# Score and expert products issued as 64-row halves of two tiles, with the dots' small operations on GpSimd

## The chip, the core and the metric

The kernel runs on one core of one Trainium2 chip. The metric is the time of one execution on the device, in microseconds (us). A core has five engines with instruction queues of their own: TensorE (PE in the profile, its weight loads PEld), VectorE (DVE), ScalarE (ACT), GpSimd (POOL) and SyncE (SP, which issues most DMAs here).

## The reference

The input x (2048 rows of 512) is normalised by row, and two branches are added to it. Branch A is attention with 32 heads of 16 columns that share one key and one value head. Branch B sends each row through 4096 experts: per head the two best of 64 keys on each of two sides are found, their four sums ranked, and the two best sums choose two experts.

```python
xn = _layernorm(x, axis=-1)
return x + _A_ref(xn, A_wq, A_wk, A_wv, A_wo) + _B_ref(xn, B_w_q, B_k1, B_k2, B_u, B_v)

# A: scores = einsum("bhqd,bkd->bhqk", q, k) * Dh**-0.5; softmax; times v; times wo
# B, per row n and head h (32 heads, dk = 128, E = 64, K = 2):
s1 = jnp.einsum("nhd,ed->nhe", q1, k1); s2 = jnp.einsum("nhd,ed->nhe", q2, k2)
i1 = jnp.argsort(-s1, axis=-1)[..., :K]; i2 = jnp.argsort(-s2, axis=-1)[..., :K]
cand = t1[..., :, None] + t2[..., None, :]         # 4 sums, of which the best 2 are kept
g = _softmax(top_s, axis=-1)
act = _gelu(jnp.einsum("nd,nhkd->nhk", xf, u[top_e]))
out = jnp.einsum("nhk,nhk,nhkd->nd", g, act, v[top_e])
```

## The kernel before

**Tiles and precision.** Rows are worked on in 16 tiles of 128. Products that must be exact are made of a high and a low part: an operand is split into two fp32r halves, and three of the four cross products are summed (`TERMS`), so a product over 512 columns takes 4 x 3 = 12 matmuls into one PSUM tile.

**Start.** Rows are normalised, transposed (`XT`), and projected to q, k and v.

**The attention loop.** Everything after that stands in one loop of 256 turns plus a tail (`att_steps`, one turn for each d). A turn issues, in this order on PE: two score products of two key blocks (`scores`, L326, 64 rows each, two side by side), the sixteen small products of the turn before with v (`pv`, L340, 32 columns each, four side by side), the second two score products, and then the fill. ScalarE takes the exponential of each score tile (L329, four per turn).

**The fill.** PE's other work is a generator (`score_thread`), which `run_scores` advances in each turn until the units it has paid for reach `done0 + (FILL - done0) * (d + 1) / half`, or 4 units in one turn (`MOST`). A matmul of the fill costs 0.235 units (`UNIT`), a full-precision block of the output projection (`block_out`) 3.6. The generator gives up control after every three matmuls. In order it contains:

- Expert scores (`item`, psc, L531): 32 items of four row tiles, 12 matmuls each. `wp_make` prepares the weights for the first eight; later items read them back (`wp_read`). DVE scans each tile with max and max_index (L544, L546); after four tiles `batch` turns the result into expert numbers and gates, partly on GpSimd (L590 to L638).
- Rows 0 to 1023 (phases 0 and 1) use their experts by gathering: `gather` (GpSimd, L976) fetches a row of u and v for each of 128 rows, `dot` (DVE, L988) makes the activation, `add` (DVE, L1023) accumulates. Between these stand three small operations on DVE per four dots (L997 to L999, queued in `CHAIN`), a tanh on ScalarE (L1004, issued in the middle of the next turn) and one more DVE operation (`weigh`, L1011).
- Rows 1024 to 2047 (phases 2 and 3) are worked through dense (`dense`): one-hot products make a gate matrix (pg, L815), and then for each of 32 blocks of 128 experts there is an activation product (pact, L733, 12 matmuls) and, after each second block, four output products (pout, L861, 6 matmuls each). The expert weights are read as fp32 and split into two halves on ScalarE and DVE (L697, L698).

**Order.** The lists `ON_ACT`, `LAST`, `LATER`, `BEHIND`, `STORES` hold functions that issue work at a set place in a later turn: `mid` runs them between the products with v and the second scores. PSUM gives three buffers to all fill tiles (`xtile`), two to attention scores. The scheduler keeps each engine's instructions in the order in which the program issues them.

Of the kernel before, what the change touches and what calls it, by code (L numbers as in the profile page):

```python
# [23 lines left out]
P = 128  # L24
# [31 lines left out]
def tile_kernel(ctx, tc, x, wq, wkv, wo, wqT, kT, uv, ub, vb, out):  # L56
# [70 lines left out]
    XT, XN, ACC, XP = {}, {}, {}, [None]  # L127
# [43 lines left out]
    def transpose_group(g):  # L171
        first = g < 1
        XT[g] = []
        for k in range(KC):
            if first:
                xt = big.tile([P, 2, 512], F32R, name="xt", tag="xt", bufs=4)
# [7 lines left out]
            XT[g].append(xt)  # L184
            if not first:
                nc.sync.dma_start(d_xt[g - 1][k], raw(xt[:]))
# [6 lines left out]
    def project_kv(g):  # L193
        p = stile("pkv")[:, 0, :]
        n = 0
        for k in range(KC):
            for a, b in TERMS:
                w = (wkv_h, wkv_l)[a]
                nc.tensor.matmul(p[:32, :], w[:, k, :], XT[g][k][:, b, :], start=n == 0, stop=n == 11)
# [21 lines left out]
    def project_q(g, wqs):  # L221
        pq = xtile("pqs")
        for r in range(KC):
            p = stile("pq")[:, 0, :]
            n = 0
            for k in range(KC):
                for a, b in TERMS:
                    nc.tensor.matmul(p, wqs[k][:, a, r * P:(r + 1) * P], XT[g][k][:, b, :],
# [282 lines left out]

    def item(n_, ti, make=()):
# [5 lines left out]
        if jb == 0:  # L518
            m8 = small.tile([P, BT, 8, 8], F32, name="m8", bufs=1)
            i8 = small.tile([P, BT, 8, 8], U32, name="i8", bufs=1)  # L520
            M8[ph, c, b], I8[ph, c, b] = m8, i8
        m8, i8 = M8[ph, c, b], I8[ph, c, b]
        p = xtile("psc")

        last = ti == TPH - 1
        more = nc_ is not None and not (ph >= NSP and c == NC - 1)
        read = more and n_ + 1 >= NC
        n = 0
        for k in range(KC):
            for a, bb in TERMS:  # L530
                nc.tensor.matmul(p, XT[g][k][:, a, j * P:(j + 1) * P], WC[n_][k][:, bb, :],  # L531
                                 start=n == 0, stop=n == 11)
                n += 1
            if read and ti == 0 and k < 2:
                wp_read(n_ + 1, range(2 * k, 2 * k + 2))
            if last and more and nph != ph:
                load_phase2_xt(nph, k)
# [5 lines left out]
        for s in range(8):  # L543
            nc.vector.max(m8[:, jb, s, :], p[:, s * E:(s + 1) * E])  # L544
        for s in range(8):
            nc.vector.max_index(i8[:, jb, s, :], m8[:, jb, s, :], p[:, s * E:(s + 1) * E])  # L546
        if jb == BT - 1:
            batch(ph, c, b)
# [14 lines left out]
    def batch(ph, c, b):  # L563
# [25 lines left out]
        G_ = nc.gpsimd  # L589
# [66 lines left out]
    def dense(DG, after):  # L656
# [4 lines left out]
        def fetch(b):  # L661
            if b < NB and b not in raws:
                rw = big.tile([P, 2, 512], F32, name="rw", tag="wqt", bufs=2)
                nc.sync.dma_start(rw[:, 0, :], ub[b])
                nc.sync.dma_start(rw[:, 1, :], vb[b])
# [27 lines left out]
        splits, halved, multiplied, halves = {}, set(), [0], {}  # L693
# [7 lines left out]
        def split(b):  # L701
            if b < NB:
                if b not in raws:
                    run(STORES)
                us = None if b < 2 else halves.pop(b) if b in halves else half_split(b, 0)
                splits[b] = us, half_split(b, 1)
                behind(lambda: halved.add(b))
                raws.pop(b)

        def later_split(b):  # L710
            def go():
                split(b)
                store(lambda: fetch(b + 2))
            on_act(go)
# [6 lines left out]
        fetch(0)  # L721
        fetch(1)
        yield 0.0
        early = []
        on_act(lambda: early.extend(half_split(b, 0) for b in range(2)))
# [3 lines left out]
        def activations(b, us, p):  # L729
            n = 0  # L730
            for k in range(KC):
                for a, c in TERMS:
                    nc.tensor.matmul(p, us[:, a, k * P:(k + 1) * P], XT[DG][k][:, c, :],  # L733
                                     start=n == 0, stop=n == 11)
                    n += 1
                yield k

        def first(b):
            p = xtile("pact")
            for k in activations(b, early[b], p):  # L740
                if k < KC - 1:
                    yield 3 * UNIT
            g, y = gate_rows(b), hh[:, b, :]
            nc.scalar.activation(y, p, AF.Square, scale=C_CUB ** 0.5)
            nc.scalar.copy(g, p)
            nc.vector.scalar_tensor_tensor(y, y, C_IN, p, op0=OP.add, op1=OP.mult)

            def go():
                nc.scalar.activation(y, y, AF.Tanh)
                behind(lambda: nc.vector.scalar_tensor_tensor(y, y, 1.0, g, op0=OP.add, op1=OP.mult))  # L750

            LATER.append(go)
            yield 3 * UNIT
# [11 lines left out]
        yield from first(0)  # L765
        rest_of_first = first(1)
        yield from islice(rest_of_first, 2)
# [37 lines left out]
        yield from rest_of_first  # L805
        onehot(1)
        for q in range(NQ):
# [28 lines left out]
            if q in (NQ - 16, NQ - 12):  # L836
                later_split((NQ - 16, NQ - 12).index(q))
            if q == NQ - 3:
                on_act(lambda: halves.__setitem__(2, half_split(2, 0)))
            if q == NQ - 3:  # L840
                quiet[0] = 3
            if q == NQ - 2:
                dense_on[0] = 3
                on_act(lambda: halves.__setitem__(3, half_split(3, 0)))
                later_split(2)
            if q == NQ - 1:
                later_split(3)
            yield 2.0
        held, ready, used = [], [], [0]

        def sums():

            used[0] += 2
            if formed[0] < used[0]:
                flush()
            for j in range(GT):
                p = xtile("pout")
                n = 0
                for wd, vs in ready:
                    for a, c in TERMS:  # L860
                        nc.tensor.matmul(p, wd[0][:, a, j * P:(j + 1) * P], vs[:, c, :], start=n == 0, stop=n == 5)  # L861
                        n += 1
                acc = ACC[GT * DG + j]
                nc.vector.tensor_add(acc, acc, p)  # L864
                yield 6 * UNIT

        stt = nc.vector.scalar_tensor_tensor
        for b in range(NB):
            wd = []
            if b > 1:  # L870
                if b not in halved:

                    yield None
                if b not in halved:
                    flush()
                p = xtile("pact")
                for k in activations(b, splits[b][0], p):
                    if k == 0:
                        store(lambda b=b: fetch_gates(b + 1))
                        if b % 2 == 0 and b > 2:  # L880
                            later_split(b + 2)
                        if b == 2:

                            store(load_totals)
                    if k == KC - 1 and b == NB - 1 and after is not None:
                        wp_read(after, range(2))
                    if b == NB - 1 and after is not None:
                        load_phase2_xt(SEQ[after][0], k)
                    if k < KC - 1:
                        yield 3 * UNIT  # L890

                if b not in fetched:
                    if b > 3 and formed[0] < b - 2:
                        flush()
                    run(STORES)
# [476 lines left out]
```

## Time and profile before

| what | value |
|---|---|
| median of 3 runs | 1929.25 us (1923.3 to 1929.8) |
| the profiled execution | 1925.78 us |
| its span | 1924.1 us |
| mean granted PE clock | 0.981 |
| busy: PE, DVE, ACT, POOL | 97%, 85%, 67%, 36% of the span |
| DMA | 491 MB, mean 255 GB/s |

The profile is of one execution; its span runs from the first to the last instruction, and the profiled time is 1.7 us longer. Groups of instructions are told by line, engine and operation, with busy time, mean duration of one and the idle time before them. Matmuls overlap each other, so the mean duration of one is longer than the distance between two.

### The profile page before, as it was taken

The page shows a single profiled execution, that of the slowest core. Times are in us where ns is not written, and L with a number is a line of the kernel's source. Part 1 is how long each engine was busy: PE and PEld are TensorE (multiplying, and loading weights), DVE is VectorE, ACT ScalarE, POOL GpSimd, SP SyncE. Part 2 cuts the span into 40 slices and gives each one's busy share as a digit, 9 for nine tenths or more (in the row PEclk, how much of TensorE's full clock was granted, in tenths as well). Part 3 has the DMA queues.
Part 4 walks back from the last instruction along what each step waited for, and adds up shares of the span by engine and source line. Part 5 has one row for each costly group of instructions (what it writes and reads, how often), then busy time and mean ns, then how long its engine had stood idle before and what let it go on. Part 6 is the DMA issues. An engine that isn't in the chain of part 4 may idle for free.

```text
span 1924.1 us, 34929 instructions
## 1 busy us (share of the span) xinstructions
PE 1863.8 (97%) x10990; PEld 991.8 (52%) x10990; DVE 1634.0 (85%) x6381; ACT 1294.2 (67%) x1803; POOL 700.8 (36%) x920
## 2 busy tenths in 40 slices
PE   6979999999999999999999999999999999999998
PEld 3634444555555554555555554555555455555553
DVE  6627787989998977999999897899988779999994
ACT  3346666655557887787877555555578777888873
POOL 1203334434452223343444444355422134344430
PEclk9989999999999899999999999999988899999999
DMA  7857789787773778888999987876736778899882
GB/s 274 315 186 278 266 272 301 279 296 251 249 246 122 233 240 249 253 288 270 287 300 309 362 287 237 280 256 220 242 105 220 249 215 292 271 284 286 282 277 84
DMA packets 234395, 491.13 MB, mean 255 GB/s; under 512 B 93396, under 2 KB 93396, under 8 KB 234204
## 3 DMA queue, kind: packets, MB, share of 16 engines
q0 software_dynamic: 73728, 268.47, 42.0%
q1 hardware_dynamic: 159240, 219.56, 34.9%
q8 instruction: 88, 1.44, 0.3%
q10 hardware_dynamic: 1236, 0.82, 0.1%
q14 instruction: 103, 0.84, 0.1%
HBM read 427.41 MB, written 56.07 MB: 251 GB/s over the span
## 4 chain that ended last, share of the span: by engine, by line
PE 85%; DMA 3%; ACT 3%; DVE 1%; issue 1%; SPq 0%; DVEq 0%; ACTq 0%
PE pv L340 24%; PE psc L531 18%; PE sc L326 17%; PE pact L733 9%; PE pout L861 9%; PE pg L815 3%; PE pwo L433 2%; ACT pt L329 2%; PE pw L486 1%; DMA wqt<-in_wqT_dram 1%; DMA dinv<-rc 1%; DMA wk<-dw 1%; PE pwt L493 0%; PE pwl L408 0%; DMA qa<-dqh 0%
## 5 line engine op out<-in xcount | busy, mean ns | idle before, releaser
L329 ACT ACTIVATE pt<-sc 128x1024 f32<-128x1024 f32 x1024 | 993.7, 1026 | 461.9 <-PE sc L326 460.5
L976 POOL DMA_INDIRECT g<-in_uv_dram,idx x512 | 556.8, 1087 | 1002.0 <-DVE xa L1023 531.0
L340 PE MATMUL pv<-pt,vaug 128*32 128x512 f32 x4096 | 516.4, 623 | 0.0
L531 PE MATMUL psc<-wk,xt 128*128 128x512 f32 x1536 | 388.7, 401 | 4.1 <-DVE wk L496 3.5
L326 PE MATMUL sc<-qa,kaug 64*128 64x512 f32 x2048 | 384.2, 451 | 8.6 <-ACT pt L329 8.4
L1023 DVE SCALAR_TENSOR_TENSOR xa<-g,w,xa 128x512 f32<-128x512 f32 x512 | 371.7, 744 | 0.1
L988 DVE CUSTOM_DVE_ANT_0 g<-g,xa 128x512 f32<-128x512 f32 x512 | 335.5, 681 | 7.4 <-DMA g<-in_uv_dram,idx 7.4
L531 PEld LDWEIGHTS psc<-wk,xt 128*128 128x128 f32 x1536 | 277.9, 188 | 107.7 <-issue 37.5
L326 PEld LDWEIGHTS sc<-qa,kaug 64*128 64x128 f32 x2048 | 155.9, 185 | 329.3 <-ACT pt L329 218.8
L340 PEld LDWEIGHTS pv<-pt,vaug 128*32 128x32 f32 x4096 | 109.6, 111 | 257.0 <-issue 255.4
L546 DVE FIND_INDEX8 i<-m,psc 128x8 uint32<-128x64 f32 x1024 | 206.3, 220 | 0.0
L733 PE MATMUL pact<-xt,wk 128*128 128x512 f32 x768 | 195.9, 400 | 0.0
L861 PE MATMUL pout<-wk,wd 128*128 128x512 f32 x768 | 194.8, 401 | 0.2 <-DVE wd L919 0.2
L544 DVE MAX8 m<-psc 128x8 f32<-128x64 f32 x1024 | 146.2, 213 | 41.1 <-PE psc L531 40.3
L861 PEld LDWEIGHTS pout<-wk,wd 128*128 128x128 f32 x768 | 140.8, 188 | 47.3 <-DVE act L988 5.5
L733 PEld LDWEIGHTS pact<-xt,wk 128*128 128x128 f32 x768 | 139.4, 188 | 48.5 <-issue 17.5
L698 DVE TENSOR_TENSOR wk<-rw,wk 128x512 fp32r<-128x512 f32 x128 | 84.8, 683 | 9.7 <-ACT wk L697 9.7
L864 DVE TENSOR_TENSOR da<-da,pout 128x512 f32<-128x512 f32 x128 | 82.8, 679 | 10.1 <-PE pout L861 10.0
L783 DVE TENSOR_TENSOR oh<-oh 128x2048 f16<-128x2048 f16 x64 | 78.0, 1219 | 0.8 <-ACT oh L759 0.6
L815 PEld LDWEIGHTS <-oh 128*128 128x128 f16 x1024 | 68.4, 162 | 13.8 <-issue 6.4
L1011 DVE SCALAR_TENSOR_TENSOR w<-gth,ga 128x4 f32<-128x4 f32 x128 | 20.4, 159 | 64.5 <-ACT gth L1004 64.0
L815 PE MATMUL pg<-oh 128*128 128x32 f16 x1024 | 73.5, 247 | 0.6 <-DVE oh L786 0.5
(159 smaller groups left out, 1411.1 us busy)
## 6 DMA issues: line engine op xcount, KB each, us to landing
wk<-dw SPq DMA_DIRECT2D x96, 512.0 KB
wqt<-in_wqT_dram SPq DMA_DIRECT2D x32, 512.0 KB
dw<-wk SPq DMA_DIRECT2D x32, 512.0 KB
rw<-in_ub_dram SPq DMA_DIRECT2D x64, 256.0 KB
rw<-in_vb_dram SPq DMA_DIRECT2D x64, 256.0 KB
gy<-dg SPq DMA_DIRECT2D x64, 256.0 KB
qa<-dqh SPq DMA_DIRECT2D x128, 64.0 KB
g<-in_uv_dram,idx POOLq DMA_INDIRECT x512, 6.0
```

The costliest lines, as they stand in the source:

```text
L326: nc.tensor.matmul(p[:, b, :], kaug[o:o + 64, kc * P:(kc + 1) * P], QA[u][o:o + 64, i, :], start=True, stop=True)
L329: nc.scalar.activation(pt, p, AF.Exp, scale=SCALE)
L340: nc.tensor.matmul(PV[u][32 * j:32 * j + 32, :], vaug[:, kc, :], pt[:, b, :], start=kc == 0, stop=kc == 15)
L531: nc.tensor.matmul(p, XT[g][k][:, a, j * P:(j + 1) * P], WC[n_][k][:, bb, :], start=n == 0, stop=n == 11)
L544: nc.vector.max(m8[:, jb, s, :], p[:, s * E:(s + 1) * E])
L546: nc.vector.max_index(i8[:, jb, s, :], m8[:, jb, s, :], p[:, s * E:(s + 1) * E])
L733: nc.tensor.matmul(p, us[:, a, k * P:(k + 1) * P], XT[DG][k][:, c, :], start=n == 0, stop=n == 11)
L815: nc.tensor.matmul(p[:, i * NB:(i + 1) * NB], oa[:, :, i], ob[:, :, i], start=True, stop=True)
L861: nc.tensor.matmul(p, wd[0][:, a, j * P:(j + 1) * P], vs[:, c, :], start=n == 0, stop=n == 5)
L976: nc.gpsimd.indirect_dma_start(out=gt, out_offset=None, in_=uv, in_offset=bass.IndirectOffsetOnAxis(ap=IDX[ph, c, ti][:, s:s + 1], axis=0))
L988: nc.vector.tensor_tensor_reduce(u, u, XN[TPH * ph + ti], scale=1.0, scalar=0.0, op0=OP.mult, op1=OP.add, accum_out=a[:, i:i + 1])
L1023: nc.vector.scalar_tensor_tensor(acc, v, w[:, i:i + 1], acc, op0=OP.mult, op1=OP.add)
```

## The change

**Half products.** Fill tiles are no longer issued as the generator goes. `item`, `first`, `sums` and the dense loop now yield a `Tile`: its list of matmuls and a function for afterwards (`done`). `run_scores` collects the tiles of a turn and hands them to `products`. That takes the last tiles of the turn, up to 12 matmuls, and issues for each matmul only the product over rows 0 to 63; beside these, one for one, it issues the products over rows 64 to 127 of the tiles that were left half done by the turn before. Tiles that do not fit, or are marked `alone`, follow as whole products. A tile of halves is therefore complete, and its `done` issued, one fill later. Score items 0 to 6 keep the old form. A turn's fill now ends at a tile's end, no longer after three matmuls.

**Dense weights.** The u half of a block is split two blocks ahead of its use, in one buffer with the v half of the block two before. The output products of a pair of blocks come as two for each of the two following blocks, no longer four in a row.

**Loads.** `XT` is one set of four tiles for all phases; a phase's last item reloads each tile's 128 columns (`load_xt`) when that tile is done. `wp_read` moves into the first tile's `done`.

**Chain.** The three DVE operations per four dots become four on GpSimd, `weigh` becomes two on GpSimd, and the tanh is issued at the end of the turn that made the dots. `CHAIN` is gone. In the last item of a dense phase, the part of `batch` that was on GpSimd runs on DVE.

```diff
+        def mm(self, i, half=None):
+            if self.p is None:
+                self.p = xtile(self.name)
+            w, v = self.steps[i]
+            n = len(self.steps)
+            if half is None:
+                nc.tensor.matmul(self.p, w, v, start=i == 0, stop=i == n - 1)
+            else:
+                o = slice(64 * half, 64 * half + 64)
+                nc.tensor.matmul(self.p, w[o], v[o], start=i == 0 and half == 0, stop=i == n - 1 and half == 1)
...
+    def products(tiles):
+
+        n, first = 0, []
+        while tiles and not tiles[-1].alone and n + len(tiles[-1].steps) <= 12:
+            n += len(tiles[-1].steps)
+            first.insert(0, tiles.pop())
+        a = [(t, i, 0) for t in first for i in range(len(t.steps))]
+        b = [(t, i, 1) for t in HALF for i in range(len(t.steps))]
+        if first or any(t.alone and t.steps for t in tiles):
+            for i in range(max(len(a), len(b))):
+                for run_ in (a, b):
+                    if i < len(run_):
+                        t, k, half = run_[i]
+                        t.mm(k, half)
+            for t in HALF:
+                t.done(t.p)
+            HALF[:] = first
+        for t in tiles:
+            t.whole()
...
+            if read and ti == 0:
+                wp_read(n_ + 1)
+            if more and nph != ph:
+                load_xt(nph, j)
...
+        tile_ = Tile("psc", steps, done)
+        if n_ >= NC - 1:
+            yield tile_
+            return
...
-        G_ = nc.gpsimd
+        G_ = V if ph >= NSP and c == NC - 1 else nc.gpsimd
...
+            return Tile("pact", activations(us_of.pop(b)), done, b == 1)
...
+            if b % 2 == 0 and b > 3:
+                yield from ready(b - 4)
+                yield from sums(b - 4, (2, 3))
+            if b % 2 and b > 1:
+                yield from ready(b - 3)
+                yield from sums(b - 3, (0, 1))
...
-            CHAIN.append(lambda: stt(q, a, C_CUB, a, op0=OP.mult, op1=OP.mult))
-            CHAIN.append(lambda: stt(y, q, C_IN, a, op0=OP.add, op1=OP.mult))
-            CHAIN.append(lambda: nc.vector.tensor_tensor(out=pairs(ga), in0=pairs(a), in1=gg, op=OP.mult))
+            V = nc.gpsimd
+            V.tensor_mul(q, a, a)
+            V.tensor_scalar(q, q, C_CUB, C_IN, op0=OP.mult, op1=OP.add)
+            V.tensor_mul(y, q, a)
+            V.tensor_tensor(out=pairs(ga), in0=pairs(a), in1=gg, op=OP.mult)
...
-            nc.vector.scalar_tensor_tensor(w, th, 1.0, ga, op0=OP.add, op1=OP.mult)
-            WT[n] = w
+        nc.gpsimd.tensor_mul(w, th, ga)
+        nc.gpsimd.tensor_add(w, w, ga)
+        WT[n] = w
...
-            if n + 1 < len(SEQ) and SEQ[n + 1][0] != ph and not (ph >= NSP and c == NC - 1):
-                yield None
...
+            if not isinstance(cost, float):
+                assert key is None
+                tiles.append(cost)
+                cost = len(cost.steps) * UNIT
             spent[0] += cost
+        products(tiles)
...
-                tanhs(d_next[0])
                 run(ON_ACT)
...
             att_steps(d, mid, fill)
+            tanhs(d_next[0])
```

More of the change, by code (lines that the diff above doesn't have):

```diff
@@ L542, in item @@
                 yield from islice(make, 1)
[L543 to L548, printed above, removed]
+        done(tile_.p)
         yield 3 * UNIT
@@ L804, in dense @@
         onehot(0)
-        yield from rest_of_first
         onehot(1)
```

330 lines of the change are left out of this document (148 added, 182 removed).

## The prediction

> **What bounds the kernel.** I read the page's busy shares and its chain first, then a table by stage, then the timeline of TensorE (PE) over single turns of the attention loop.
>
> ```profile
> span 1924.1 us, 34929 instructions
> PE 1863.8 (97%) x10990; PEld 991.8 (52%) x10990; DVE 1634.0 (85%) x6381; ACT 1294.2 (67%) x1803; POOL 700.8 (36%) x920
> PE 85%; DMA 3%; ACT 3%; DVE 1%; issue 1%; SPq 0%; DVEq 0%; ACTq 0%
> ```
>
> PE is busy 97% of the span and carries 85% of the chain that ended last. The table (columns: PE, PEld, DVE, ACT, POOL, clock, DMA share, GB/s) covers score fill, dense fill, score fill, dense fill:
>
> ```profile
> 353.00:590.00 237.00, 235.39 (x1345) 130.49 (x1341) 220.48 (x1415) 137.26 (x168) 112.54 (x201) 1.00 0.76 265
> 744.00:1066.00 322.00, 321.39 (x1818) 177.09 (x1818) 297.58 (x695) 252.19 (x356) 132.45 (x118) 1.00 0.89 285
> 1066.00:1400.00 334.00, 333.14 (x1873) 179.18 (x1877) 301.06 (x1845) 193.90 (x237) 153.86 (x251) 1.00 0.78 266
> 1560.00:1890.00 330.00, 329.70 (x1863) 180.42 (x1855) 305.45 (x716) 257.09 (x365) 130.60 (x115) 1.00 0.86 271
> ```
>
> PE is full in all four; VectorE (DVE) follows at 90 to 93%. So a turn lasts as long as PE's work in it. One turn with 15 fill products, the next with 18; then a turn without fill:
>
> ```profile
> 513.38 0.73 PE L326 MATMUL sc<-qa,kaug 64*128 64x512 f32 x4
> 514.04 1.92 PE L340 MATMUL pv<-pt,vaug 128*32 128x512 f32 x16
> 515.89 0.73 PE L326 MATMUL sc<-qa,kaug 64*128 64x512 f32 x4
> 516.56 3.70 PE L531 MATMUL psc<-wk,xt 128*128 128x512 f32 x15
> 520.18 0.73 PE L326 MATMUL sc<-qa,kaug 64*128 64x512 f32 x4
> ...
> 523.36 4.38 PE L531 MATMUL psc<-wk,xt 128*128 128x512 f32 x18
> 527.67 0.73 PE L326 MATMUL sc<-qa,kaug 64*128 64x512 f32 x4
> 528.33 1.06 PE L340 MATMUL pv<-pt,vaug 128*32 128x512 f32 x8
> ```
>
> ```profile
> 373.67 1.92 PE L340 MATMUL pv<-pt,vaug 128*32 128x512 f32 x16
> ...
> 377.22 0.51 PE L326 MATMUL sc<-qa,kaug 64*128 64x512 f32 x2 [0.97 <-ACT pt L329]
> 378.14 0.50 PE L326 MATMUL sc<-qa,kaug 64*128 64x512 f32 x2 [0.41 <-ACT pt L329]
> 378.57 0.64 PE L340 MATMUL pv<-pt,vaug 128*32 128x512 f32 x4
> ```
>
> The first turn is 520.18 - 513.38 = 6.80 us, the second 527.67 - 520.18 = 7.49: three products more cost 0.69, so a full 128-row fill product is 0.228. Without its 15 products a turn is 6.80 - 3.42 = 3.38. Of that, sixteen pv are four groups of (1.92 - 1.06)/2 = 0.43, together 1.72; eight sc are four pairs, and a second pair adds 0.73 - 0.50 = 0.23, together 0.92. What is left, 0.74, belongs to the four places where the row or column form of the products changes (sc to pv, pv to sc, sc to fill, fill to sc): 0.185 each. The turn without fill lasts 378.57 - 373.67 = 4.90, not 3.38: there PE waits for ScalarE's exponentials (ACT pt). 4.90 is a floor under every turn.
>
> **The change, part by part.**
>
> *Mode changes removed.* A fill that holds only half products keeps the 64-row form of sc on both sides: two of the four changes go, 2 x 0.185 = 0.37. A fill that also runs a whole tile keeps both. How often? A turn's budget is (948 - 17)/256 = 3.64 units at 0.235 per product, 15.5 products, and a tile is now taken whole. Score tiles have 12 products (2.82 units), so a fill takes one or two, 1.29 on average. The 25 items in the new form have 100 tiles: 78 fills, 55 with a single tile, which then runs as halves only. In the dense stage a block is one pact (12) and two pout (6 each); by the budget the fills go round through [pout, pout], [pact, pout], [pout, pact]. Only the first has no whole tile. Worked through turn by turn this gives 20 and 21 such fills. Sum: 96 x 0.37 = -36 us. Items 0 to 6 stay as they are.
>
> *Halves without a partner.* `products` takes the last tiles up to 12 products as first halves and runs them beside the second halves left from the fill before; the shorter list leaves slots with one half. In the round above the lists are 12 and 12, 6 and 12, 12 and 6: 36 slots, and 18 whole products beside them, for what was 48 products. Six slots are lost per three fills: 168 in the two dense stages, 6 more where `first(1)` is alone. A lone half is not in the trace.
>
> ```profile
> L531 PE MATMUL psc<-wk,xt 128*128 128x512 f32 x1536 | 388.7, 401 | 4.1 <-DVE wk L496 3.5
> L326 PE MATMUL sc<-qa,kaug 64*128 64x512 f32 x2048 | 384.2, 451 | 8.6 <-ACT pt L329 8.4
> L531 PEld LDWEIGHTS psc<-wk,xt 128*128 128x128 f32 x1536 | 277.9, 188 | 107.7 <-issue 37.5
> L326 PEld LDWEIGHTS sc<-qa,kaug 64*128 64x128 f32 x2048 | 155.9, 185 | 329.3 <-ACT pt L329 218.8
> ```
>
> From below it is 0.114, half a product; from above 0.228. A 64-row product is not shorter than a 128-row one (451 ns against 401) and its weight load is as long (185 against 188), so I take 0.228: 174 x 0.228 = +40 us; with the low end +20.
>
> *Pairs.* 2,112 slots hold halves. The sc pair at 0.23 says that a slot with two halves costs what a whole product costs: 0. The low end is the load alone, 0.185: -91. The high end, 0.24, is +25.
>
> *ScalarE's floor.* In the dense stages ACT is busy 252.2/322 = 78% of turns of about 6.9 us, 5.4 us; four exponentials are 4.1, so 1.3 of other work stands on top of what the 4.90 floor holds. A turn of twelve slots would need 3.38 + 12 x 0.228 - 0.37 = 5.75 on PE, less than 4.90 + 1.3. Of the 0.37 saved there between none and all is lost; I take 0.15 in 41 turns, +6 (0 to +15).
>
> *Chain on GpSimd (POOL).* Three small DVE operations and `weigh` become six POOL ones, per four slots, 128 times.
>
> ```profile
> L1011 DVE SCALAR_TENSOR_TENSOR w<-gth,ga 128x4 f32<-128x4 f32 x128 | 20.4, 159 | 64.5 <-ACT gth L1004 64.0
> L999 DVE TENSOR_TENSOR ga<-act,gg 128x4 f32<-128x4 f32 x128 | 20.2, 158 | 0.0
> L998 DVE SCALAR_TENSOR_TENSOR gy<-gq,act 128x4 f32<-128x4 f32 x128 | 20.2, 158 | 1.6
> L997 DVE SCALAR_TENSOR_TENSOR gq<-act 128x4 f32<-128x4 f32 x128 | 20.1, 157 | 0.4
> L630 POOL TENSOR_TENSOR e<-e,cond 128x16 f32<-128x16 f32 x32 | 13.5, 421 | 2.5
> L976 POOL DMA_INDIRECT g<-in_uv_dram,idx x512 | 556.8, 1087 | 1002.0 <-DVE xa L1023 531.0
> ```
>
> DVE loses 81 us of work and 64 of waiting for the tanh; PE sets the turn, so this is worth 0. POOL gains 768 x 0.42 = 323 us beside 701, which fits its idle time, but two orders change. (The last item's list of 13 operations goes the other way, twice, to DVE: 26 x 0.16 = 4 us, beside PE, 0.) First, ScalarE's tanh now stands before the next turn's exponentials and waits for four POOL operations. Second, the two POOL operations that form w stand behind the fill's `batch` on POOL.
>
> ```profile
> 503.97 0.08 DVE L988 DVE_READ_ACCUMULATOR2_ANT act<- 128x1 f32 x1
> ...
> 510.19 1.40 DVE L1023 SCALAR_TENSOR_TENSOR xa<-g,w,xa 128x512 f32<-128x512 f32 x2
> ```
>
> ```profile
> 507.18 1.94 ACT L329 ACTIVATE pt<-sc 128x1024 f32<-128x1024 f32 x2 [2.35 <-PE sc L326]
> ```
>
> ```profile
> 508.13 0.31 POOL L590 CAST fi<-i 128x64 f32<-128x64 uint32 x1 [2.20 <-DVE i L546]
> ...
> 514.09 0.46 POOL L638 TENSOR_TENSOR da<-hi,ii 128x32 f32<-128x32 f32 x2
> ```
>
> Tanh: the fourth dot ends at 504.05; four POOL operations at 0.42 end at 505.7 to 506.0, the next exponential starts at 507.18, so the tanh is hidden here with a microsecond to spare; where a gather (1.09) is still in front of the chain it is just late: +2 us in all (0 to 128 x 0.3 = +38). w: with such a batch (508.13 to 514.55) in front, w comes at about 515.5, while DVE wants it at 510.19: DVE stands 5 us, and behind it wait the scan of the next score tile and so PE's third PSUM buffer. Of some 29 items with such a batch about half meet a w (one w per two turns, one batch per three); 15 x 5 = 75 us of DVE standing, against the 64 that go. PE feels only what exceeds its buffers, about half a microsecond per stop: +8 (0 to +75).
>
> *Reads, order, queues.* `wp_read` moves from inside an item's first tile to its `done`, a fill later, behind PE on SP's queue.
>
> ```profile
> 499.86 5.77 SPq L504 DMA_DIRECT2D wk<-dw  x4
> ```
>
> The next item starts some 21 us after this one (48 products, 15.5 in a turn of 6.8), and the issue falls about 9 us later than now, a turn and a half of it; the four reads, 2 MB at the 265 GB/s of this stage, need 8. That fits with 4 us to spare: +1 (0 to 17 x 2 = +34 where gathers take half the bandwidth). The phase's `XT` columns are loaded a tile's time ahead in 16 DMAs instead of 4 on SP, hidden behind three tiles. The `yield None` at a phase's end goes, and with it a 4.90 turn, while the dense start has a turn more: -2. Halving dense weights two blocks ahead has the same copies and subtractions (0); at most eight of the eight wk buffers are held.
>
> **Sum.** -36 + 40 + 6 + 2 + 8 + 1 - 2 = +19 against the profiled execution's 1925.8: 1945. The median of the runs shown is 1929.25, so I forecast 1944, 0.8% above it. What a measurement of this kernel can tell from no change is about 0.5%, 9.6 us: below 1919.6 is faster, above 1938.9 slower.
>
> **The rivals.** *Faster: slots with halves run under a product's time.* If the weight load of one row half hides under the other half's product, a slot falls to between 0.185 and 0.228; at 0.21, 2,112 x 0.018 = -38: 1906. It decides the sign from 0.216 down. For it: the load (0.188) is most of the 0.228. Against it: sc pairs are already of this form and stand 0.23 apart, and 0.188 of load in a 0.228 step means that full products already load beside products. [...]
>
> *Slower still: waits.* The late w, the late tanh and the floor pass to PE in larger part: half of 75, 15 of 38, all of 15 make 67 where I count 16: 1995 at the worst, 1970 at half the excess. For it: DVE at 93% in the score stage. Against it: it also loses 145 us.
>
> *Nothing.* Mode changes and lost slots cancel, the waits stay hidden: 1925.8 - 36 + 40 - 2 = 1928.
>
> **How the numbers follow.** My sum 0.45 (its own range 1931 to 1958), waits 0.20, nothing 0.20, fast slots 0.15. The range leaves out a few per cent beyond the fast slots and the upper waits: 1908 to 1974. Faster: the fast slots and little of the third, 0.17. Slower: the waits and three quarters of my sum, 0.52. Within 0.5%: 0.31.
>
> **What would show it.** Right: turns in the score stage with twelve slots at 5.7 us, those with a whole tile besides near 8.9; in the dense stage products of 64 rows at half the rate where one list is longer. Slots spaced under 0.22 prove the rival. Rows of DVE waiting for POOL's w, or ScalarE's gth waiting for POOL, give the waits. The forecast is wrong if the fills divide otherwise than counted, or if a lone half costs less than a pair.

## The result, and the profile after

The changed kernel takes 2032.72 us (median of 4 runs, 2028.88 to 2040.56) beside 1928.82 us for the kernel before on the same chip (4 runs): 1.055 times as long, 95% interval 1.0509 to 1.0591. The forecast was 1944, with a range up to 1974. From the page of the profile after, the lines that answer to the first three shown of before:

```profile
span 2034.6 us, 39210 instructions
PE 1897.9 (93%) x12940; PEld 1064.4 (52%) x12940; DVE 1600.6 (79%) x5899; ACT 1291.9 (63%) x1803; POOL 955.7 (47%) x1658
PE 58%; DVE 17%; POOL 5%; ACT 5%; issue 4%; DMA 4%; SPq 0%; ACTq 0%; POOLq 0%; DVEq 0%
```

PE carried 85% of the chain that ended last and now carries 58%; DVE has gone from 1% to 17% and POOL to 5%. PE waits for others, which it hardly did before. The table by stage, columns as in the prediction, cut at the same turns in both kernels (score fill, dense fill, score fill, dense fill), first before, then after:

```profile
346.04:590.27 244.23, 242.62 (x1387) 134.49 (x1385) 226.62 (x1449) 142.19 (x175) 113.67 (x203) 1.00 0.76 267
709.35:1066.52 357.17, 356.56 (x1990) 191.43 (x1988) 321.60 (x745) 277.14 (x390) 141.55 (x126) 1.00 0.88 282
1066.52:1399.68 333.16, 332.30 (x1868) 178.87 (x1866) 300.22 (x1841) 193.52 (x237) 153.86 (x251) 1.00 0.78 266
1531.31:1887.38 356.07, 355.77 (x1987) 191.19 (x1985) 324.10 (x757) 276.82 (x390) 137.69 (x122) 1.00 0.86 270
```

```profile
346.36:606.50 260.14, 244.43 (x1796) 147.65 (x1794) 219.49 (x1362) 142.72 (x176) 131.95 (x300) 0.96 0.75 250
748.61:1135.79 387.18, 369.40 (x2475) 209.32 (x2474) 314.83 (x626) 276.28 (x392) 215.49 (x312) 1.00 0.83 264
1135.79:1489.48 353.69, 332.13 (x2417) 193.81 (x2415) 294.55 (x1751) 193.63 (x237) 187.02 (x391) 0.98 0.75 250
1609.82:1997.51 387.69, 370.38 (x2470) 211.18 (x2469) 317.50 (x630) 277.08 (x393) 214.22 (x312) 1.00 0.79 250
```

The two score stages are 16 and 21 us longer, the two dense stages 30 and 32. In all four PE now stands for 16 to 22 us, where it stood for about one. The one-hot stages between them differ by +23 and -11 us; there the granted clock moved too, from 0.93 and 0.86 to 0.83 and 0.96.

The work of PE itself is what the prediction counted. One turn of the dense stage with halves only, from the timeline of the changed kernel, and the turn behind it:

```profile
828.38 1.92 PE L341 MATMUL pv<-pt,vaug 128*32 128x512 f32 x16
...
830.24 0.72 PE L327 MATMUL sc<-qa,kaug 64*128 64x512 f32 x4
...
831.04 0.39 PE L528 MATMUL pout<-wk,wd 64*128 64x512 f32 x1
831.04 0.39 PE L528 MATMUL pact<-xt,wk 64*128 64x512 f32 x1
831.04 0.18 PEld L528 LDWEIGHTS pout<-wk,wd 64*128 64x128 f32 x1
831.04 0.18 PEld L528 LDWEIGHTS pact<-xt,wk 64*128 64x128 f32 x1
831.27 0.39 PE L528 MATMUL pout<-wk,wd 64*128 64x512 f32 x1
831.27 0.39 PE L528 MATMUL pact<-xt,wk 64*128 64x512 f32 x1
...
834.16 1.92 PE L341 MATMUL pv<-pt,vaug 128*32 128x512 f32 x16
...
836.71 2.95 PE L528 MATMUL pout<-wk,wd 64*128 64x512 f32 x18
...
840.07 1.27 DVE L900 TENSOR_TENSOR da<-da,pout 128x512 f32<-128x512 f32 x2
840.80 1.88 PE L525 MATMUL pact<-xt,wk 128*128 128x512 f32 x7 [1.13 <-DVE da L900]
```

Two halves start together, and the next two 0.23 us later; the next weights are loaded while they run (0.18 us each beside products of 0.39). The turn is 834.16 - 828.38 = 5.78 us, against 5.75 by the sum. The turn behind it shows what the sum left out: the halves of three pout tiles end at 839.66, and the whole pact tile that follows starts only at 840.80, after DVE has added up one of those tiles. Three pout tiles are alive, and pact needs a fourth buffer where there are three. Each dense stage has seven turns of this form; their medians are 10.2 and 10.5 us, in place of 8.85.

A turn of the score stage, same view:

```profile
470.17 2.91 PE L528 MATMUL psc<-wk,xt 64*128 64x512 f32 x24
...
475.96 0.46 POOL L693 TENSOR_TENSOR da<-hi,ii 128x32 f32<-128x32 f32 x2
...
476.38 0.65 POOL L1035 TENSOR_TENSOR gq<-act 128x4 f32<-128x4 f32 x1
...
477.54 0.20 POOL L1038 TENSOR_TENSOR ga<-act,gg 128x4 f32<-128x4 f32 x1
477.62 0.21 ACT L1043 ACTIVATE gth<-gy 128x4 f32<-128x4 f32 x1 [5.48 <-POOL gy L1037]
477.73 1.92 ACT L330 ACTIVATE pt<-sc 128x1024 f32<-128x1024 f32 x2
...
478.79 1.71 PE L327 MATMUL sc<-qa,kaug 64*128 64x512 f32 x4 [3.39 <-ACT pt L330]
...
479.68 0.75 DVE L1056 SCALAR_TENSOR_TENSOR xa<-g,w,xa 128x512 f32<-128x512 f32 x1 [2.71 <-POOL w L1047]
...
480.30 5.28 PE L528 MATMUL psc<-wk,xt 64*128 64x512 f32 x24
```

ScalarE's tanh waits 5.48 us, the exponentials stand behind it, and PE waits 3.39 us for them. This turn lasts 15.6 us in place of 8.91. PE's wait is only half of that: behind it the granted clock is 0.55 (480 to 486 us), and 24 half products take 5.28 us where the 24 of the turn before took 2.91. The list of waits over the whole changed kernel (us in total, times, longest):

```profile
ACT gth L1043 <- POOL gy L1037: 95.2, 42, 5.5
DVE xa L1056 <- POOL w L1047: 51.4, 30, 3.7
PE sc L327 <- ACT pt L330: 44.0, 48, 3.5
PE pact L525 <- DVE da L900: 15.9, 13, 4.3
PE pout L525 <- DVE gy L946: 10.0, 10, 2.4
```

Held against the prediction's own turn (3.38 plus 0.228 a slot, 0.37 less with halves alone, 4.88 at least), the turns of the four stages exceed it by 25.0, 26.6, 31.8 and 25.9 us, waits and slower clock together; before it was 0.8, 4.1, 1.1 and 3.7.

### The profile page after: what moved, and what is told of

Same layout as the page of the kernel before. It is cut to its first block, busy times and chain, and to the rows that moved or that the text cites. A ratio compares the mean times of both kernels' runs of the same rounds, so it can differ in the third digit from the quotient of the medians.

```text
span 2034.6 us, 39210 instructions
## 1 busy us (share of the span) xinstructions
PE 1897.9 (93%) x12940; PEld 1064.4 (52%) x12940; DVE 1600.6 (79%) x5899; ACT 1291.9 (63%) x1803; POOL 955.7 (47%) x1658
## 4 chain that ended last, share of the span: by engine, by line
PE 58%; DVE 17%; POOL 5%; ACT 5%; issue 4%; DMA 4%; SPq 0%; ACTq 0%; POOLq 0%; DVEq 0%
PE pv L341 16%; PE sc L327 11%; PE psc L528 7%; PE pact L528 6%; PE psc L525 5%; DVE xa L1056 4%; ACT pt L330 3%; DVE i L587 3%; PE pg L859 3%; PE pout L525 3%; PE pact L525 3%; DVE g L1026 2%; DVE m L585 2%; DMA g<-in_uv_dram,idx 2%; PE pwo L434 2%
## 5 line engine op out<-in xcount | busy, mean ns | idle before, releaser
L1056 DVE SCALAR_TENSOR_TENSOR xa<-g,w,xa 128x512 f32<-128x512 f32 x512 | 371.2, 744 | 52.0 <-POOL w L1047 51.4
L1035 POOL TENSOR_TENSOR gq<-act 128x4 f32<-128x4 f32 x128 | 73.2, 572 | 383.2 <-DVE act L1026 383.0
L528 PE MATMUL psc<-wk,xt 64*128 64x512 f32 x1896 | 247.7, 400 | 3.1 <-DVE i L587 1.6
L528 PE MATMUL pact<-xt,wk 64*128 64x512 f32 x1128 | 235.6, 391 | 0.0
L528 PEld LDWEIGHTS psc<-wk,xt 64*128 64x128 f32 x1896 | 196.8, 191 | 40.5 <-DVE i L587 2.7
L528 PE MATMUL pout<-wk,wd 64*128 64x512 f32 x876 | 193.2, 395 | 4.8 <-DVE da L900 3.5
L528 PEld LDWEIGHTS pact<-xt,wk 64*128 64x128 f32 x1128 | 179.6, 186 | 31.3
L525 PE MATMUL psc<-wk,xt 128*128 128x512 f32 x588 | 156.1, 406 | 5.2 <-DVE wk L497 3.6
L528 PEld LDWEIGHTS pout<-wk,wd 64*128 64x128 f32 x876 | 141.6, 185 | 21.8 <-DVE da L900 4.4
L525 PEld LDWEIGHTS psc<-wk,xt 128*128 128x128 f32 x588 | 104.4, 188 | 53.3 <-issue 23.8
L525 PE MATMUL pout<-wk,wd 128*128 128x512 f32 x330 | 90.9, 412 | 12.3 <-DVE gy L946 10.0
```

Of the source, the lines that this page charges most:

```text
L525: nc.tensor.matmul(self.p, w, v, start=i == 0, stop=i == n - 1)
L528: nc.tensor.matmul(self.p, w[o], v[o], start=i == 0 and half == 0, stop=i == n - 1 and half == 1)
L1056: nc.vector.scalar_tensor_tensor(acc, v, w[:, i:i + 1], acc, op0=OP.mult, op1=OP.add)
```

## The experiments

Every ratio is against runs of the kernel before on the same chip, with its 95% interval. One per cent is 19 us.

### The chain on GpSimd

First the chain went back to DVE in the changed kernel, all else left; then it alone was put into the kernel before.

```diff
 # a_chain_dve: the changed kernel; b_chain_pool: the kernel before with the opposite edit
-            V = nc.gpsimd
-            V.tensor_mul(q, a, a)
...
+            CHAIN.append(lambda: stt(q, a, C_CUB, a, op0=OP.mult, op1=OP.mult))
...
-        nc.gpsimd.tensor_mul(w, th, ga)
-        nc.gpsimd.tensor_add(w, w, ga)
+            nc.vector.scalar_tensor_tensor(w, th, 1.0, ga, op0=OP.add, op1=OP.mult)
...
+                tanhs(d_next[0])
                 run(ON_ACT)
...
-            tanhs(d_next[0])
...
```

> The changed kernel with the dots' chain, the weighing and the tanh's place as before (DVE, middle of the next turn); half products stay. Theory 1 (order on GpSimd): in the score stage ScalarE's tanh waits for the chain, which stands behind batch on GpSimd, and the exponentials and PE wait behind it; the 57 us that turns of the score stages exceed their products by go, and some 20 us of GpSimd's delays elsewhere at most: 1955 to 1980. Theory 2 (lumps): whole tiles at a time make DVE's scans and so PE's PSUM buffers late, wherever the chain runs: at least 2020. The dense stage's excess stays under both.

> The kernel before with this one part of the change: chain and weighing on GpSimd, tanh at a turn's end. Theory 1: slower than before by 40 to 60 us, 1970 to 1990, in the score stages, and ScalarE's gth waits for GpSimd. Theory 2: within 10 us of before, since no tile is taken whole.

Measured: 1992.11 us, 1.0335 (1.0283 to 1.0387), and 1956.98 us, 1.0145 (1.0075 to 1.0215), each between its two ranges. The chain's move costs 2.15% in the changed kernel, about 41 us, and 28 in the kernel before. It is a large part of the 104, and not all of it. In the changed kernel the excess of the score turns falls from 56.8 us to 3.1 with it. The two score stages become 54.6 us shorter: PE stands for 35.8 us less, and its busy time for the same products falls by 18.9, most of that by the granted clock, which was 0.96 and 0.98 there and is now 0.99 and 1.00.

Two more kernels ask why. One puts only the tanh back into the middle of the next turn; the other takes `batch`, which stands ahead of the chain on GpSimd, to DVE.

```diff
 # a_tanh_mid
+                tanhs(d_next[0])
                 run(ON_ACT)
...
-            tanhs(d_next[0])
```

> The changed kernel with the tanh back in the middle of the turn; the chain stays on GpSimd, and so do the two operations that form w. Theory 1 (the chain's 41 us come from the tanh, which stands in front of the next turn's exponentials while it waits for GpSimd): 1990 to 2005, and ACT gth's wait for POOL gy disappears or comes where it holds no exponential. Theory 2 (they come from w, which comes late behind GpSimd's batch and holds VectorE): 2020 to 2045, with DVE xa waiting for POOL w as long as before or longer.

```diff
 # a_batch_dve
-        G_ = V if ph >= NSP and c == NC - 1 else nc.gpsimd
+        G_ = V
```

> The changed kernel with the operations of the score batch taken from GpSimd to VectorE; chain and w stay on GpSimd. Theory 1 (the chain costs because it queues behind a batch of some 6 us on GpSimd, and tanh and w come late by that): ACT gth's wait for POOL gy falls from 95 us to under 40 and the time to 1995 to 2012. Theory 2 (the chain is late by its own length, six GpSimd operations of 0.27 to 0.57 us and the gathers between them): the wait stays above 70 and the time between 2025 and 2050, since VectorE gets more work.

Measured: 2010.71 us, 1.038 (1.0336 to 1.0424), 6 us above its first range, and 2042.55 us, 1.0583 (1.0548 to 1.0618), within its second. Their waits, first with the tanh in the middle, then with the batch on DVE:

```profile
ACT gth L1043 <- POOL gy L1037: 24.9, 13, 3.8
DVE xa L1056 <- POOL w L1047: 81.0, 54, 5.8
```

```profile
ACT gth L1043 <- POOL gy L1037: 100.8, 43, 5.5
```

The tanh's place accounts for 1.7 of the 2.15%. That w comes later still (81.0 us of waiting in place of 51.4) costs little once no exponential stands behind the tanh: what is left of the 2.15% is 0.45, which lies within the intervals. The batch is not the cause alone: with it off GpSimd the wait stays. In the changed kernel, 27 of the tanh's waits are over 1 us, 87.7 us together. Of these some 35 lie between the start of the chain and the tanh (1.3 us each), 28 between the end of the fourth dot and the start of the chain, and the other 24 or so are the dot's own lateness; the split is a rough estimate. With the batch on DVE the middle share is under 5 of 95.8 and the dot's own lateness over 40. So the batch gave its delay to DVE, and the dots behind it came late instead. Since that kernel loads DVE more (238.52 and 315.95 us of work in the two score stages, in place of 219.49 and 294.55), what the batch alone is worth stays open.

### Halves

Three kernels change which fills run as halves.

```diff
 # a_no_halves: the changed kernel, every fill product whole
-        while tiles and not tiles[-1].alone and n + len(tiles[-1].steps) <= 12:
+        while False and n + len(tiles[-1].steps) <= 12:
 # a_dve_densewhole: a_chain_dve, all tiles of the dense stage alone
-                yield Tile("pact", activations(us_of.pop(b)), done)
+                yield Tile("pact", activations(us_of.pop(b)), done, True)
...
 # a_dve_one_first: a_chain_dve, one tile at most as first halves
-        while tiles and not tiles[-1].alone and n + len(tiles[-1].steps) <= 12:
+        while not first and tiles and not tiles[-1].alone and n + len(tiles[-1].steps) <= 12:
```

> The changed kernel with every tile issued as whole products in its own turn; order, loads and GpSimd's chain as changed. Theory 1: lone slots (-40) and the dense stage's waits for a fourth PSUM buffer (-45) go, mode changes come back (+36), the waits for GpSimd stay: 1975 to 1995. Theory 2, in its form that the delay of a tile by one fill makes the lumps: 1925 to 1945.

> The changed kernel with the chain on DVE as before and with the dense stage's tiles as whole products; half products remain in the score stages alone. Theory 1, with lone slots and PSUM buffers as the dense stage's loss: 55 turns save 0.37 us each, and nothing else remains: 1900 to 1915, faster than before. Theory 2: waits in turns of two tiles stay: 1930 to 1960.

> The changed kernel with the chain on VectorE again (1992.1 us), and now a fill takes at most one tile as first halves; a second tile of the fill runs whole. At most three fill tiles are then alive on PE at once (one half old, one half new, one whole), where the changed kernel needs four. The slots of a dense round stay 54 (18 in each of its three fills), but no fill of it holds halves alone any more, so 41 fills lose their 0.37: +15. Theory 1 (in the dense stage a whole tile stands and waits for the adds that empty two half tiles, because PE has three buffers): the rows of pact and pout waiting for DVE's da and gy shrink from some 45 us to under 10, and the time is 1960 to 1975. Theory 2 (the waits come from halves being emptied late and together, however many are alive): 1985 to 2010.

Measured: 2006.32 us, 1.0404 (1.0341 to 1.0466); 1951.28 us, 1.0124 (1.0072 to 1.0177); 1997.45 us, 1.034 (1.0298 to 1.0383). Halves in the dense stages cost 3.35 - 1.24 = 2.1%, 41 us. The first two came out above their first ranges, the second inside its other one: something beside halves and chain still cost some 40 us. The third lies in its second range and left the time where it was, though the waits moved as the first theory said; its stages say why. The dense stage of phase 2 and the score stage behind it, first with two tiles as first halves, then with one:

```profile
719.14:1114.98 395.84, 372.52 (x2475) 211.20 (x2474) 323.86 (x750) 276.69 (x392) 140.56 (x128) 0.98 0.83 262
1114.98:1437.79 322.81, 322.81 (x2417) 192.14 (x2415) 299.90 (x1838) 193.58 (x237) 149.06 (x251) 1.00 0.79 264
```

```profile
721.40:1099.60 378.20, 374.43 (x2404) 209.23 (x2403) 324.99 (x751) 278.55 (x392) 141.86 (x128) 1.00 0.85 268
1099.60:1441.71 342.11, 330.45 (x2411) 194.31 (x2409) 300.43 (x1837) 193.40 (x237) 150.48 (x251) 0.98 0.77 256
```

With three tiles alive the dense stage is 17.6 us shorter. The seven turns with 18 pout halves and a whole pact, 10.57 us in the one kernel where their work is 8.85, are gone; seven turns with 12 halves and a whole pact in the other last 7.54, where their work is 7.48; PE's wait for `da` before pact (16.4 us) is out of the list, and that for `gy` before pout falls from 11.8 to 4.4. The fourth buffer was a cause. The other dense stage gained only 2.3. In both, the turns with pairs alone (14 and 16, of 5.8 us) went, most of them to turns of 7.5; in the first, the stage's last two turns also became 7.5 us shorter. And 19 us came back in the next stage. Its first turn, 16.86 us in place of 7.48, waits for the weights of the new phase's scores:

```profile
1103.18 0.39 PE L528 MATMUL pout<-wk,wd 64*128 64x512 f32 x1
1107.80 1.65 PE L528 MATMUL psc<-wk,xt 64*128 64x512 f32 x3 [4.23 <-DMA wk<-dw]
1110.91 1.64 PE L528 MATMUL psc<-wk,xt 64*128 64x512 f32 x3 [1.46 <-DMA wk<-dw]
1112.48 2.92 PE L525 MATMUL pout<-wk,wd 128*128 128x512 f32 x6
```

That is 9.4 us. Another 8.0 are one later turn (16.81 us in place of 8.85), behind a wait that the trace doesn't name (last section). To run a tile's second half directly behind its first, which would keep fewer tiles alive, was not tried.

### The order: a tile at a time

What is left of the change without halves and without the chain:

```diff
 # a_dve_no_halves: a_chain_dve, every fill product whole
-        while tiles and not tiles[-1].alone and n + len(tiles[-1].steps) <= 12:
+        while False and n + len(tiles[-1].steps) <= 12:
```

> The changed kernel with the chain on VectorE again and every fill product whole; what is left of the change is the order (a tile at a time, dense weights halved two blocks ahead, loads in columns). Beside the variant with halves in the score stages alone (1951.3) it says what halves are worth there. Theory 1 (a score fill that holds halves only saves the two mode changes, 78 x 0.37 = 29 at most, some of it lost on other floors): 1965 to 1980. Theory 2 (halves are worth nothing in a score stage): 1946 to 1956. In both, what it lies above the kernel before is the price of the order.

Measured: 1977.12 us, 1.0232 (1.0199 to 1.0264), in the first range. The order alone costs 2.3%, 45 us, where the prediction had -1. Halves in the score stages are worth 2.32 - 1.24 = 1.1%, 21 us. Two kernels divide the 45.

```diff
 # c_no_halves: a_dve_no_halves with the dense stage of before (products three at a time, old order of blocks, all batches partly on GpSimd)
 # a_dve_fine: a_dve_no_halves, new order of blocks, but products three at a time
+    def fine(name, steps, done):
+        t = Tile(name, steps, done)
+        for i in range(len(steps)):
+            t.mm(i)
+            if i == len(steps) - 1:
+                done(t.p)
+            if i % 3 == 2:
+                yield 3 * UNIT
...
-                yield Tile("pact", activations(us_of.pop(b)), done)
+                yield from fine("pact", activations(us_of.pop(b)), done)
```

> The dense stage of before and the chain on VectorE; the score stages take whole products, a tile at a time, with the loads of the change. Beside the same kernel with halves (1942.3) it prices the halves in score stages a second time, and beside the variant with the changed dense order and no halves (1977.1) it prices that order. Theory 1 (prices add up: halves save 26 in the score stages, the score stages' own order costs the rest): 1962 to 1975, and the dense order then costs only some 10. Theory 2 (the dense order carries the loss, and with it gone taking a tile at a time costs little): 1930 to 1948.

> The changed dense order (activation weights halved two blocks ahead, pact then two and two pout, loads as changed), but its products go out three at a time again, so that fills hold 12 to 18 of them as before; the chain on VectorE, whole products everywhere, score stages a tile at a time. It stands between the variant with the same order and whole tiles (ratio 1.0232) and the one with the dense stage of before (1.0049). Theory 1 (the dense stage loses because a fill takes whole tiles: fills of 6 that stand on a floor of 6.3 us, fills of 24, and loads that are asked for a fill later): 1.003 to 1.010, and the waits of the stage's ends, DVE for gy and for rc, are gone. Theory 2 (it loses by the new order of blocks and loads): 1.016 to 1.024, with those waits as long as before.

Measured: 1936.81 us, 1.0049 (1.0027 to 1.0071), in the second range, and 1953.31 us, 1.011 (1.0086 to 1.0135), just above the first. So the tile-wise score stages cost 0.5% (9 us), the kernel with the new order of blocks 0.6% more (12), and whole tiles in the dense fills another 1.2% (24). Of the 9, some 8 are the first two turns of the second score stage in c_no_halves (14.61 and 7.05 us in place of 7.48 and 6.12), which wait for wk. Of the 12, the two dense stages themselves hold only 4.2; the rest lies in other stages and isn't shown to be the order's. The dense stage of phase 2, whole tiles, then three at a time:

```profile
720.75:1106.44 385.69, 366.76 (x1984) 194.56 (x1982) 325.74 (x755) 277.44 (x391) 143.27 (x127) 0.97 0.85 265
```

```profile
725.91:1086.95 361.04, 357.23 (x1988) 191.25 (x1986) 323.29 (x753) 278.03 (x391) 138.89 (x127) 1.00 0.88 279
```

That is 24.7 us, as much as the 1.2%. With whole tiles, fills of 6, 12, 18 and 24 products take the place of fills of 12, 15 and 18. Those of 6 last 6.37 us in the median in place of 4.88, some 7 us over the stage. More lies at the two ends. At its start DVE waits for the gates (in the list of waits for 720 to 1080 us, whole tiles), at its end for the sums of the softmax, rc (in the list for the whole kernel):

```profile
DVE gy L946 <- DMA gy<-dg: 14.4, 4, 9.9
DVE rc L379 <- DMA rc<-dsum: 12.7, 2, 9.6
```

A turn at the start lasts 15.29 us where before it was 6.85, one at the end 16.76 against 7.78. In each PE stands first (3.2 us for the exponentials, 5.0 for `wd`), and the granted clock is 0.97 over the stage, where it is 1.00 three at a time. Three at a time these turns are 11.5 and 7.45, and the two waits over the whole kernel are shorter, though not gone: 8.1 us in place of 23.3 for gy, 4.8 in place of 12.7 for rc.

The last two kernels ask whether halves in the score stages alone gain.

```diff
 # c_score_halves: c_no_halves with halves in the score stages
 # c_reads_early: the same; weights of an item read when the item two before it ends,
 # and the first item after a dense stage three products at a time
...
-            if read and ti == 0:
+            if read and ti == 0 and not early and not own_wait:
                 wp_read(n_ + 1)
+            if ti == TPH - 1 and n_ >= NC - 1 and not dense_last(n_) and n_ + 2 < len(SEQ) and not dense_last(n_ + 1):
+                wp_read(n_ + 2)
...
-        if n_ >= NC - 1:
+        if n_ >= NC - 1 and not own_wait:
             yield tile_
...
```

> Halves in the score stages only, the chain on VectorE, and the dense stage as it was before, products three at a time and in the old order. Theory 1 (halves save their mode changes in the score stages, and everything else of the change costs): 1905 to 1918, faster than before. Theory 2 (what the halves save is given back elsewhere, by the clock or by reads that come later): 1922 to 1940.

> Halves in the score stages, the dense stage of before, the chain on VectorE; and the weights of an item are read a fill earlier (as the last tile of the item two before it is emptied), and the first item after a dense stage takes its products three at a time as before, so that it needs its weight quarters one after the other. Theory 1 (what the halves save is lost again at the start of the second score stage, to reads that come late: 13.4 and 7.0 us turns there instead of 6.1 and 8.2): 1915 to 1930, and psc waits for DMA wk under 1 us. Theory 2 (the loss there is not of the reads): 1935 to 1948.

Measured: 1942.28 us, 1.0046 (1.0025 to 1.0067), and 1921.26 us, 0.9983 (0.9956 to 1.0011). The first missed both of its ranges: no gain over whole products (1.0049). The second came out as its first theory said. The second score stage, with the reads of the change, then early:

```profile
1076.00:1419.06 343.06, 332.44 (x2393) 192.88 (x2391) 300.17 (x1838) 193.41 (x237) 149.71 (x251) 0.99 0.77 257
```

```profile
1073.63:1397.99 324.36, 323.67 (x2357) 191.24 (x2355) 299.09 (x1838) 193.57 (x237) 149.33 (x251) 1.00 0.79 270
```

From 343 us it falls to 324, against 333 in the kernel before. Only 7.2 of these 18.7 us belong to the reads: the first two turns, 13.39 and 7.00 us in place of 7.48 and 5.75. A tile taken as a whole wants all four quarters of its weights in one fill, and at the phase's start they are still under way. With the reads early no wait of psc for wk is left in the list; which of the two edits did it was not divided. Another 11.4 us are three later turns (11.64, 12.92 and 10.25 in place of 8.85, 8.85 and 5.75), behind waits that the trace doesn't name and that only some chips show (last section). They also stand against what the halves gain over whole products in this pair, whose other kernel ran on chip 4. With the reads early, the time is not to be told from the kernel before: no version here is shown to beat it.

## Why the prediction was wrong

It had the sign. Its sum, +19 us, was 85 short of the 104 measured; the forecast of 1944 added the 19 to the profiled execution and not to the median, which would have given 1948. From kernel before to changed kernel, the ratios above give a ladder: tile-wise score stages +9, new order of dense blocks +12, whole tiles in dense fills +24, halves in the score stages -21, halves in the dense stages +41, the chain +41. That is 106 us, beside 104 measured. It is one order of steps, and the terms depend on each other: the chain costs 28 us in the kernel before, 33 in the changed kernel without halves (1.0404 less 1.0232) and 41 with them.

- **Mode changes removed (-36).** Right in size. A turn of twelve slots takes 5.75 us with halves and 6.13 whole, and the score stages' share, 55 x 0.37 = 20, measured 21. A second pair of kernels, c_score_halves and c_no_halves, measured nothing, with 11.4 us of the unnamed waits in the first of them alone.
- **Halves without a partner (+40)** and **pairs (0).** Right. A turn with six pout halves beside twelve pact halves lasts 5.75 us, as long as one with twelve pairs, and pairs stand 0.23 apart. The rival of fast slots falls with that, though its premise, loads beside products, is seen: at 831.04 us loads of 0.18 us for both halves run beside products of the same rows.
- **ScalarE's floor (+6).** Small, as forecast: dense turns of twelve slots have a median of 5.77 us in both stages, 0.02 over the sum's 5.75 where I took 0.15.
- **What the halves' terms left out.** By them halves in the dense stage should cost -15 + 38 + 6 = 29; they cost 41. The text held no count of tiles alive at once: two pout half new, one half old and a whole pact want four buffers. The fourteen turns of that form are 1.4 and 1.6 us too long in the median of the two stages, some 21 us. That is more than the 12 missing, but the kernel without halves stalls too, at its own stage ends.
- **Chain on GpSimd (+10).** Mis-sized: 41. The step that failed is "hidden here with a microsecond to spare", read from one turn. In the kernel before it was a fair reading (the fourth dot ends some 4 us ahead of the next turn's first exponential in the median of 128, and less than 1.4 ahead in under one in ten). But the slack doesn't survive the change: where w or a scan holds DVE, the next dots come late, then the chain, the tanh, the exponentials and PE. The queue behind `batch` was charged to w alone, and it stands before the tanh as well. Nor did the sum price what PE's waits do to its clock: of the 54.6 us that the chain costs the score stages, 18.9 are PE's busy time and not its standing.
- **Reads, order, queues (-1).** The step that was wrong by most: 45. It looked at `wp_read` by bandwidth in the middle of a stage, and it priced "a tile is now taken whole" by slots alone. The runs show what whole tiles do besides: uneven fills on a floor, and at the starts and ends of stages loads that come late for what needs them at once, with PE slower behind long waits (granted clock 0.55 behind one of 3.39 us in the changed kernel, 0.51 behind one of 4.23 in a_dve_one_first).
- **The rival of waits (1970)** had the kind right, PE waiting for what it had not waited for, and not its places: it knew the late w, the late tanh and the floor, and neither the buffers nor the order.

Not settled: the one-hot stages' net +12 us beside their changed clock, and the new order's 0.6%, which no run divided. The steps of 12 and of -21 each compare a kernel timed on a chip with unnamed waits and one without; these waits take some 8 us of the second score stage in a_dve_fine and in a_dve_no_halves, so both steps are less sure than their intervals.

## What to carry to other kernels

When a change makes the work coarser (a tile where there were three matmuls), count three things per turn besides the engine's time: how many buffers are alive at once, what the smallest and the largest fill cost, and when each load is asked for and needed. An operation put in front of the critical engine's feed must be costed for the worst turn and with the delays that it causes itself, since its slack in the old trace was made by the old order. Change one thing at a time where the terms of a sum are of both signs: here -21 and +41 came from the same edit in two stages.

## What was not expected of the hardware

The long waits of PE shown here cost more than their length. After the 4.23 us wait for wk shown above (same kernel, table by stretches):

```profile
1099.00:1106.00 7.00, 4.58 (x37) 2.10 (x36) 4.76 (x13) 3.88 (x4) 2.21 (x2) 1.00 1.03 406
1106.00:1116.00 10.00, 6.74 (x16) 3.97 (x16) 0.56 (x1) 0.00 (x0) 0.00 (x0) 0.51 0.92 290
```

the granted clock is 0.51 over the next 10 us, and the six whole products at 1112.48 take 2.92 us where six in a row at full clock take 1.65 (c_score_halves, 1078.52 us). The clock falls while PE still waits: it is 1.00 from 1099 to 1106 us, and if it stands at 0.50 behind the fall, as it does in the changed kernel from 479 to 485 us, a mean of 0.51 puts the fall at some 1106.2 us. By this estimate that is 2.6 us after the last product (1103.18 and 0.39 long) and 1.6 before the next (1107.80).

In a_dve_one_first, c_score_halves, a_dve_no_halves and a_dve_fine the exponentials also waited, up to 7.3 us at a time, for something that the trace doesn't name, when the products they wait for stood as issued (13.7 us in three waits in c_score_halves). As far as these traces show, it goes with the chip: in all five traces taken on chips 10 and 13 (these four and a_tanh_mid) the list of waits puts 15 to 34 us of the exponentials' waiting down to no instruction (`remote` or `issue`), and none of seven others has such a row, c_reads_early on chip 4 among them. The kernel before was timed on chips 10 and 13 too (medians 1932.4 and 1931.3 us, beside 1925.6 and 1928.2 on chips 4 and 8), but not traced there. What it is stays open, and so does how much of it the ratios hold.

The chain's six operations on 128 x 4 elements took 572, 408, 390, 444, 265 and 297 ns on GpSimd in the changed kernel, where the prediction had 420 each; the three on DVE had taken 157 or 158.
